# A fused GELU layer and its gradients: the plain loads of the first block, moved from SyncE's DMA queue to GpSimd's

## The chip, the cores and the metric

The kernel runs on one core of a Trainium2 chip. The metric is the device time of one execution in microseconds. All tensors are bf16; products are accumulated in f32.

## The reference

```python
# x [1, 2048, 448], w1 [448, 1792], b1 [1792], w2 [1792, 448], b2 [448], grad_out like x
def _fwd_reference(x, w1, b1, w2, b2):
    h = jnp.einsum("bsd,df->bsf", x, w1) + b1
    h = jax.nn.gelu(h, approximate=True)
    return jnp.einsum("bsf,fd->bsd", h, w2) + b2

_out, _vjp = jax.vjp(_fwd_reference, x, w1, b1, w2, b2)
return (_out, *_vjp(grad_out))     # out, and the gradients of x, w1, b1, w2, b2
```

## The kernel before

The 2048 rows of x are cut into four blocks of 512, and the 1792 hidden features into seven pairs of 128-wide tiles. One step is one pair of one block, so the first part has 28 steps. In a step TensorE makes `pu` (x times w1, transposed: features on partitions) and `pq` (grad_out times w2, transposed); ScalarE and VectorE turn these into `hT` (the GELU) and `ghT` (the gradient at the hidden layer). Out of hT and ghT TensorE also makes the rows of the output and of x's gradient ("units", bank `ps`), which are stored through GpSimd's queue. The second part makes the weight gradients from hT, ghT, x and grad_out; the change does not touch it.

448 is three times 128 plus 64. The last 64 rows of w1 are a tensor of their own on the chip, `wt1`, and the half products with them (line 237) use 64 partitions. For pq, grad_out and w2 are read shifted by 64, so that the half tile comes first.

What each product needs on the chip: `xT` and `gT` (x and grad_out, transposed by the DMA), `w1_f` and `wt1` (w1 as it is), `w2T` (w2 transposed), `w2_sb` (w2 as it is, for the output units) and `w1T_sb` (w1 transposed, for the units of x's gradient). The loads of the first block come in pieces by columns or tiles of the hidden features, because the pairs are taken in the order `FP = [1, 2, 3, 4, 5, 6, 0]`: the first step takes columns 256 to 512, the second 512 to 768, the third 768 to 1024, and the last 0 to 256.

The order of all instructions is written out by hand (`tc.manual_schedule()`): each engine runs its instructions in program order and waits for semaphores. DMAs are issued by three engines in their own queues: SyncE (SP), ScalarE (ACT) and GpSimd (POOL). In the profile q1 is SyncE's DMA queue, q10 ScalarE's and q0 GpSimd's. DMAs of SyncE and ScalarE share eight completion semaphores, so that one waits, before it is issued, until the one eight places back has landed; GpSimd's have eight of their own, used in the same way.

In the kernel before, SyncE issues nearly all loads of the first block, transposes and plain loads interleaved (lines 142 to 168): x's two halves, w1 512:768, w1 768:1024, w2 tiles 2:4, gT, w2T 256:512, and so on up to w1T (line 167) and the second block's gT. ScalarE issues w1 256:512 (line 143). GpSimd issues only b1 (line 139) before the first output rows are ready.

On TensorE the first steps run in this order: pu of step 0 (line 216, and its half product, line 237), pu of step 1, pu of step 2 (w1 768:1024), four pairs of matmuls of output units for step 0 (`pieces`, line 372, with w2 tiles 2:4), the half products of pu of step 2 and of pq of step 0 (line 237: `wt1`, `gT`, `w2T`), the rest of pq of step 0 (line 273), units for step 1, and so on. w1T is first used at step 7 (line 372). VectorE's last instruction of a step, `dve_gh` (line 343), takes pq and writes ghT.

The names in the profile leave out digits: `w_f` is w1_f, `wt` is wt1, `w_sb` is w2_sb, `b_rows` is b1_rows and `b_bc` is b2_bc; a line 121, 122, 125 or 129 is that of the loading helper.

Of the kernel before, what the change touches and what calls it, by code (L numbers as in the profile page):

```python
# [19 lines left out]
def kernel(  # L20
# [15 lines left out]
    nc = tc.nc  # L36
    P = 128
    B, S, D = x.shape
    F = w1.shape[1]
    assert (B, S, D, F) == (1, 2048, 448, 1792)  # L40
    NS = S // P
    NF = F // P
    KF = D // P
    DL = D - KF * P
    SB = 512
# [8 lines left out]
    ROW0 = [SB, 2 * SB, 3 * SB, 0]  # L54
# [4 lines left out]
    x2 = x.rearrange("b s d -> (b s) d")  # L59
# [18 lines left out]
    b2_bc = const.tile([P, D], BF16, name="b2_bc")  # L78
    row0 = const.tile([P, P], BF16, name="row0")
    w1_f = const.tile([P, KF, F], BF16, name="w1_f")  # L80
    w2T = const.tile([P, KF + 1, F], BF16, name="w2T")
    wt1 = const.tile([P, F], BF16, name="wt1")
# [12 lines left out]
    xT, gT = {}, {}  # L95

    def wide(src, r0, n, shift):
        return bass.AP(src.tensor, src.offset + r0 * D - shift, [[D, n], [1, (KF + 1) * P]])

    def load_x(b):  # L100
        t = blk.tile([P, KF + 1, SB], BF16, name="xT", tag="xT")
        r0 = ROW0[b]
        if b in WIDE:
            nc.sync.dma_start_transpose(out=t[:], in_=wide(x2, r0, SB, 0))  # L104
        else:
            nc.sync.dma_start_transpose(out=t[:, 0:KF, :], in_=x2[r0:r0 + SB, 0:KF * P])
            nc.sync.dma_start_transpose(out=t[:, KF, :], in_=x2[r0:r0 + SB, D - P:D])
        xT[b] = t

    def load_g(b):  # L110
        t = blk.tile([P, KF + 1, SB], BF16, name="gT", tag="gT")
        r0 = ROW0[b]
        if b in WIDE:
            nc.sync.dma_start_transpose(out=t[:], in_=wide(g2, r0, SB, DL))  # L114
        else:
            nc.sync.dma_start_transpose(out=t[:, 1:KF + 1, :], in_=g2[r0:r0 + SB, DL:D])
            nc.sync.dma_start_transpose(out=t[:, 0, :], in_=g2[r0:r0 + SB, 0:P])
        gT[b] = t

    def load_w1(eng, f0, f1):  # L120
        eng.dma_start(out=w1_f[:, :, f0:f1], in_=w1[0:KF * P, f0:f1].rearrange("(kt p) f -> p kt f", p=P))  # L121
        eng.dma_start(out=wt1[0:DL, f0:f1], in_=w1[KF * P:D, f0:f1])  # L122

    def load_w2(eng, t0, t1):
        eng.dma_start(out=w2_sb[:, t0:t1, :], in_=w2[t0 * P:t1 * P, :].rearrange("(ft p) d -> p ft d", p=P))  # L125

    def load_w2T(f0, f1):
        if f0 > 0:
            nc.sync.dma_start_transpose(out=w2T[:, :, f0:f1], in_=wide(w2, f0, f1 - f0, DL))  # L129
        else:  # L130
            nc.sync.dma_start_transpose(out=w2T[:, :, 16:f1], in_=wide(w2, 16, f1 - 16, DL))
            nc.sync.dma_start_transpose(out=w2T[:, 1:KF + 1, 0:16], in_=w2[0:16, DL:D])
            nc.sync.dma_start(out=w2T[DL:P, 0, 0:16], in_=w2[0:16, 0:DL].rearrange("f d -> d f"))

    nc.vector.memset(zero[:], 0.0)
    nc.gpsimd.memset(b1_rows[:], 0.0)
# [2 lines left out]
    nc.gpsimd.dma_start(out=b1_rows[0:NF, :], in_=b1.rearrange("(ft p) -> ft p", p=P))  # L139
    xT[0] = blk.tile([P, KF + 1, SB], BF16, name="xT", tag="xT")  # L140
    halves = [slice(0, SB // 2), slice(SB // 2, SB)]
    nc.sync.dma_start_transpose(out=xT[0][:, :, halves[0]], in_=wide(x2, ROW0[0], SB // 2, 0))
    load_w1(nc.scalar, 256, 512)
    nc.sync.dma_start_transpose(out=xT[0][:, :, halves[1]], in_=wide(x2, ROW0[0] + SB // 2, SB // 2, 0))
    warm = stg.tile([P, 1], F32, name="warm", tag="warm", bufs=1)
    nc.scalar.activation(out=warm[:], in_=zero[:, 0:1], func=ACT.Gelu_apprx_tanh)
    load_w1(nc.sync, 512, 768)
    load_w1(nc.sync, 768, 1024)
    load_w2(nc.sync, 2, 4)
    load_g(0)  # L150
    load_w2T(256, 512)
    load_w2(nc.sync, 4, 6)
    load_w1(nc.sync, 1024, 1280)
    load_w2T(512, 768)
    load_w2(nc.sync, 6, 8)
    load_w1(nc.sync, 1280, 1536)
    load_w2T(768, 1280)
    load_w2(nc.sync, 8, 12)
    load_w1(nc.sync, 1536, F)
    load_w1(nc.sync, 0, 256)  # L160
    load_w2(nc.sync, 12, NF)
    load_w2(nc.sync, 0, 2)
    load_w2T(1280, F)
    nc.sync.dma_start(out=b2_bc[:], in_=b2.rearrange("(o d) -> o d", o=1).to_broadcast((P, D)))
    load_x(1)
    load_w2T(0, 256)
    nc.sync.dma_start_transpose(out=w1T_sb[:], in_=w1[:, :])
# [256 lines left out]
    loads = {6: ("x", 2), 8: ("g", 2), 10: ("x", 3), 11: ("g", 3)}  # L424
# [44 lines left out]
    for i in range(1, NSINGLE):  # L469
        f = i + LEAD  # L470
# [271 lines left out]
```

## Time and profile before

| | |
|---|---|
| median of 3 runs | 271.88 us (271.28 to 272.45) |
| the profiled execution | 272.33 us, its span 270.5 us |
| TensorE (PE) busy | 263.7 us, 97% of the span |
| VectorE (DVE), ScalarE (ACT) busy | 176.1 and 139.3 us |
| GpSimd (POOL) busy | 39.7 us |
| DMA queue of SyncE, of GpSimd, of ScalarE | 36.43, 4.27 and 3.44 MB |
| chain that ended last | PE 82%, SyncE's queue 12%, DMA 4% |
| granted TensorE clock | 1.00 |

The profile is one execution. Times in it count from the start of its span. "Busy" leaves out the time of queues: an issue by SyncE ("SPq") has a duration, but is the time in which the queue is taken, and the data lands some microseconds later. In the chain of waits each row is followed back to what released it. A row of waits has the waiting engine, tile and line, then what it waited for, and then the sum in us, the number of waits and the longest one. In a timeline row the bracket tells how long the engine was idle before it, and what ended this.

### The profile page before, as it was taken

The numbers are of one execution on the slowest core, as the hardware profiler recorded it, in microseconds if no ns is written. First come the engines' busy times: TensorE is split into PE (matmuls) and PEld (weight loads), VectorE is DVE, ScalarE is ACT, GpSimd is POOL, SyncE is SP. The second block draws the span as 40 slices with busy tenths as digits, with TensorE's granted clock in tenths as the row PEclk, the third lists the DMA queues.
The fourth block names the chain that finished last, engine by engine and source line by source line (L and its number), as shares of the span: only waits on it lengthen the run. The fifth ranks groups of instructions, "written<-read, shape, count | busy, mean of one in ns | idle before, by whom it ended". The sixth has DMA issues, their size and how long they took to land.

```text
span 270.5 us, 4721 instructions
## 1 busy us (share of the span) xinstructions
PE 263.7 (97%) x1941; PEld 148.0 (55%) x1948; DVE 176.1 (65%) x208; ACT 139.3 (51%) x163; POOL 39.7 (15%) x50
## 2 busy tenths in 40 slices
PE   8999998999999999999999999999999999999995
PEld 7334343444445665555457888874444665555554
DVE  1689999799999779696798930309999992000000
ACT  2898899689995867968676520012111211111111
POOL 1000004011002020110202021221510007900000
PEclk9999999999999999999999999999999999999999
DMA  7999989999999995162642439999311111999851
GB/s 161 207 186 252 180 168 186 252 261 183 250 257 218 266 210 130 61 166 58 168 101 93 78 56 249 368 242 271 92 40 39 41 29 45 195 224 227 202 126 34
DMA packets 112965, 44.44 MB, mean 164 GB/s; under 512 B 92032, under 2 KB 111824, under 8 KB 112944
## 3 DMA queue, kind: packets, MB, share of 16 engines
q1 hardware_dynamic: 106352, 36.43, 63.2%
q0 software_dynamic: 1824, 4.27, 5.2%
q10 hardware_dynamic: 4768, 3.44, 4.1%
q8 instruction: 15, 0.25, 0.4%
q14 instruction: 6, 0.05, 0.1%
HBM read 7.23 MB, written 14.23 MB: 79 GB/s over the span
## 4 chain that ended last, share of the span: by engine, by line
PE 82%; SPq 12%; DMA 4%; issue 1%; ACT 0%
PE ps L237 23%; PE ps_v L694 16%; PE ps_w L662 13%; PE pq L237 9%; PE pu L237 8%; DMA w1T_sb<-in_w_dram 4%; PE ps L372 4%; SPq L129 4%; PE pu L216 3%; PE pq L273 2%; PE ps_w L673 2%; SPq L125 1%; SPq L104 1%; SPq L121 1%; SPq L122 1%; SPq L114 1%
## 5 line engine op out<-in xcount | busy, mean ns | idle before, releaser
L311 ACT ACTIVATE U<-pu,b1T 128x512 bf16<-128x512 f32 x55 | 33.9, 687 | 20.3 <-PE pu L237 20.1
L343 DVE SCALAR_TENSOR_TENSOR ghT<-Z,pq 128x1024 bf16<-128x1024 bf16 x28 | 33.9, 1221 | 14.2 <-PE pq L237 11.5
L386 POOL DMA_DIRECT2D out_dram<-st x32 | 19.1, 602 | 161.4 <-ACT st L383 107.6
L694 PE MATMUL ps_v<-g_nat,h_nat 128*128 128x448 bf16 (+1 forms) x240 | 42.6, 340 | 0.0
L237 PE MATMUL pq<-gT,w2T 64*128 64x512 bf16 x242 | 36.2, 376 | 0.6 <-DMA w2T<-in_w_dram 0.5
L662 PE MATMUL ps_w<-gh_nat,x_nat 128*128 128x512 bf16 (+1 forms) x192 | 36.5, 352 | 0.0
L237 PE MATMUL ps<-w1T_sb,ghT 64*128 64x448 bf16 x336 | 33.9, 349 | 0.0
L694 PEld LDWEIGHTS <-h_nat 128*128 128x128 bf16 x240 | 23.3, 98 | 19.3 <-DMA out_dram<-st 0.3
L237 PE MATMUL ps<-w_sb,hT 64*128 64x448 bf16 x336 | 33.7, 349 | 0.0
L329 ACT ACTIVATE Z<-Z 128x2048 bf16<-128x2048 bf16 (+1 forms) x18 | 27.5, 1528 | 7.7 <-DVE Z L325 7.6
L648 DVE TENSOR_TENSOR acc<-acc,gh_nat 128x1792 f32<-128x1792 f32 x14 | 30.0, 2142 | 0.5
L662 PEld LDWEIGHTS <-x_nat 128*128 128x128 bf16 x192 | 18.7, 98 | 17.9 <-issue 0.4
L237 PEld LDWEIGHTS <-ghT 64*128 64x128 bf16 x336 | 23.5, 94 | 8.7
L320 ACT ACTIVATE A<-U 128x1024 bf16<-128x1024 bf16 (+1 forms) x19 | 27.7, 1457 | 0.7 <-DVE U L313 0.4
L317 ACT ACTIVATE hT<-U 128x1024 bf16<-128x1024 bf16 (+1 forms) x20 | 27.7, 1391 | 0.2
L237 PEld LDWEIGHTS <-hT 64*128 64x128 bf16 x336 | 20.4, 94 | 11.9
L697 ACT CAST st<-ps_v 128x448 bf16<-128x448 f32 (+1 forms) x15 | 7.6, 507 | 34.8 <-PE ps_v L694 34.8
L383 ACT CAST st<-ps 128x448 bf16<-128x448 f32 x20 | 9.8, 532 | 29.0 <-PE ps L237 27.6
L216 PE MATMUL pu<-xT,w_f 128*128 128x512 bf16 (+1 forms) x100 | 22.6, 366 | 0.6 <-DMA xT<-in_x_dram 0.4
L237 PEld LDWEIGHTS <-w2T 64*128 64x128 bf16 x248 | 18.0, 94 | 8.7 <-DMA w2T<-in_w_dram 1.1
L665 ACT CAST st<-ps_w 128x512 bf16<-128x512 f32 (+1 forms) x12 | 6.4, 533 | 28.9 <-PE ps_w L662 28.9
L237 PE MATMUL pu<-xT,w_f 64*128 64x512 bf16 x144 | 20.5, 376 | 0.0
(52 smaller groups left out, 256.0 us busy)
## 6 DMA issues: line engine op xcount, KB each, us to landing
hT_dram<-hT SPq DMA_DIRECT2D x28, 256.0 KB, 3.0
out_dram<-st POOLq DMA_DIRECT2D x32, 112.0 KB, 3.5
x_nat<-in_x_dram SPq DMA_DIRECT2D x1, 1792.0 KB, 9.5
g_nat<-in_grad_out_dram SPq DMA_DIRECT2D x1, 1792.0 KB, 14.4
out_dram<-st ACTq DMA_DIRECT2D x13, 112.0 KB, 3.4
w_f<-in_w_dram SPq DMA_DIRECT2D x6, 192.0 KB, 4.1
out_dram<-st ACTq DMA_DIRECT2D x9, 128.0 KB, 1.7
w_sb<-in_w_dram SPq DMA_DIRECT2D x5, 224.0 KB, 4.2
```

The source lines that it names most:

```text
L129: nc.sync.dma_start_transpose(out=w2T[:, :, f0:f1], in_=wide(w2, f0, f1 - f0, DL))
L216: nc.tensor.matmul(PU[f][a][:, rs], lhsT=w1_f[:, kt, cols(p, a)], rhs=xT[b][:, kt, rs], start=(kt == 0 and rs.start == 0), stop=False, ski ...
L237: mm = nc.tensor.matmul(ps, lhsT=w, rhs=m, start=start, stop=stop, tile_position=(hf.start, 0), skip_group_check=True)
L311: nc.scalar.activation(out=dst, in_=PU[f][a][:], func=ACT.Identity, bias=bias)
L317: nc.scalar.activation(out=rows(hT, r), in_=part(U4, r), func=ACT.Gelu_apprx_tanh)
L320: nc.scalar.activation(out=part(A4, ks), in_=part(U4, ks), func=ACT.Square, scale=math.sqrt(3.0 * GELU_A * GELU_C))
L329: nc.scalar.activation(out=z, in_=z, func=ACT.Tanh, scale=-1.0 / 3.0)
L343: nc.vector.scalar_tensor_tensor(out=rows(ghT, [k]), in0=part(Z4, [k]), scalar=1.0, in1=PQ[k][:], op0=ALU.add, op1=ALU.mult)
L386: nc.gpsimd.dma_start(out=(out2 if self.kind == "o" else gx2)[r:r + P, :], in_=st[:, 0:D])
L648: nc.vector.tensor_tensor(out=v, in0=in0, in1=gh_nat[:, b, :, j, :], op=ALU.add)
L662: nc.tensor.matmul(ps[:, 0:n * P], lhsT=x_nat[:, st_, kt * P:(kt + 1) * P], rhs=gh_nat[:, b, ft0:ft0 + n, j, :], start=(st_ == 0), stop=(s ...
L694: nc.tensor.matmul(ps[:, 0:w], lhsT=h_nat[ft][:, st_, :], rhs=g_nat[:, st_, h * w:(h + 1) * w], start=(st_ == 0), stop=(st_ == NS - 1))
```

## The change

The plain loads from w1 768:1024 onwards leave SyncE's queue and are issued by GpSimd. In front of them stands an empty instruction on GpSimd, which waits until the first half of x has landed. w1's 64 last rows are loaded for columns 768 to 1792 in one DMA instead of four. b2's load and the piece of w2T with 2-byte elements (16 rows, 64 columns) move to the end of GpSimd's list. SyncE's queue is left with the transposes in their old order, and w1 512:768.

```diff
@@ load_w2T
-            nc.sync.dma_start(out=w2T[DL:P, 0, 0:16], in_=w2[0:16, 0:DL].rearrange("f d -> d f"))
@@ the loads of the first block
-    nc.sync.dma_start_transpose(out=xT[0][:, :, halves[0]], in_=wide(x2, ROW0[0], SB // 2, 0))
+    first = nc.sync.dma_start_transpose(out=xT[0][:, :, halves[0]], in_=wide(x2, ROW0[0], SB // 2, 0))
     load_w1(nc.scalar, 256, 512)
...
     load_w1(nc.sync, 512, 768)
-    load_w1(nc.sync, 768, 1024)
-    load_w2(nc.sync, 2, 4)
+    landed = nc.gpsimd.nop()
+    tc.add_manual_dep(landed.ins, first.ins.name, mybir.DependencyInfo(mybir.DependencyClass.Sync, mybir.DependencyReason.DATA),
+                      reason="plain loads behind x")
+    nc.gpsimd.dma_start(out=w1_f[:, :, 768:1024], in_=w1[0:KF * P, 768:1024].rearrange("(kt p) f -> p kt f", p=P))
+    nc.gpsimd.dma_start(out=wt1[0:DL, 768:F], in_=w1[KF * P:D, 768:F])
+    load_w2(nc.gpsimd, 2, 4)
+    load_w2(nc.gpsimd, 4, 6)
+    nc.gpsimd.dma_start(out=w1_f[:, :, 1024:1280], in_=w1[0:KF * P, 1024:1280].rearrange("(kt p) f -> p kt f", p=P))
+    load_w2(nc.gpsimd, 6, 8)
+    nc.gpsimd.dma_start(out=w1_f[:, :, 1280:1536], in_=w1[0:KF * P, 1280:1536].rearrange("(kt p) f -> p kt f", p=P))
+    load_w2(nc.gpsimd, 8, 12)
+    nc.gpsimd.dma_start(out=w1_f[:, :, 1536:F], in_=w1[0:KF * P, 1536:F].rearrange("(kt p) f -> p kt f", p=P))
+    load_w1(nc.gpsimd, 0, 256)
+    load_w2(nc.gpsimd, 12, NF)
+    load_w2(nc.gpsimd, 0, 2)
+    nc.gpsimd.dma_start(out=b2_bc[:], in_=b2.rearrange("(o d) -> o d", o=1).to_broadcast((P, D)))
+    nc.gpsimd.dma_start(out=w2T[DL:P, 0, 0:16], in_=w2[0:16, 0:DL].rearrange("f d -> d f"))
     load_g(0)
     load_w2T(256, 512)
-    load_w2(nc.sync, 4, 6)
-    load_w1(nc.sync, 1024, 1280)
     load_w2T(512, 768)
-    load_w2(nc.sync, 6, 8)
-    load_w1(nc.sync, 1280, 1536)
     load_w2T(768, 1280)
-    load_w2(nc.sync, 8, 12)
-    load_w1(nc.sync, 1536, F)
-    load_w1(nc.sync, 0, 256)
-    load_w2(nc.sync, 12, NF)
-    load_w2(nc.sync, 0, 2)
     load_w2T(1280, F)
-    nc.sync.dma_start(out=b2_bc[:], in_=b2.rearrange("(o d) -> o d", o=1).to_broadcast((P, D)))
     load_x(1)
     load_w2T(0, 256)
     nc.sync.dma_start_transpose(out=w1T_sb[:], in_=w1[:, :])
```

## The prediction

> **What bounds the kernel now.** The page's first lines say that TensorE is busy for 97% of the span, so only its waits can be won. I asked for these waits, and they are short:
>
> ```profile
> PE 263.7 (97%) x1941; PEld 148.0 (55%) x1948; DVE 176.1 (65%) x208; ACT 139.3 (51%) x163; POOL 39.7 (15%) x50
> PE ps L372 <- DMA w1T_sb<-in_w_dram: 1.1, 1, 1.1
> PE pq L237 <- DMA w2T<-in_w_dram: 0.5, 2, 0.3
> PE pu L216 <- DMA xT<-in_x_dram: 0.4, 1, 0.4
> ```
>
> The 6.8 us in which TensorE is not busy are mostly start and end. DMA waits that the change can touch are w1T (1.09 us, ending at 46.05) and two for w2T (0.24 and 0.28, at 13.05 and 18.47): **1.61 us in all, the most it can win**. x's own wait stays, since nothing ahead of it moves. The chain of waits shows why w1T is late: from 0.7 to 34.5 us it runs through SyncE's queue, issue after issue with 0.04 us between. The queue is bound by issuing, and the transposes stand behind the plain loads:
>
> ```profile
> 4.70 0.58 SPq L121
> 5.86 0.59 SPq L125
> 6.49 2.84 SPq L114
> 9.37 1.30 SPq L129
> ...
> 33.84 0.66 SPq L133
> 34.54 11.47 DMA w1T_sb<-in_w_dram
> ```
>
> When data is needed I read from TensorE's timeline (start, duration, line): the first users of w1 columns 768 to 1024, of w2 rows 2:4, and of gT with the first w2T part.
>
> ```profile
> 9.51 1.47 PE L216 MATMUL pu<-xT,w_f 128*128 128x512 bf16 x6
> 10.82 1.68 PE L372 MATMUL ps<-w_sb,hT 128*128 128x448 bf16 x8
> 13.05 0.39 PE L237 MATMUL pq<-gT,w2T 64*128 64x512 bf16 x1 [0.24 <-DMA w2T<-in_w_dram]
> ```
>
> By the DMA view, narrowed to these issues, w1 768 is issued at 4.70 and lands 3.4 us later (8.1, 1.4 us early); w2 2:4 is issued at 5.86 and lands 3.6 later (9.4, also 1.4 early). So the early plain loads have 1.4 us of slack, and the two early w2T parts have none.
>
> **The change, part by part.** *Off SyncE.* 18 plain issues leave its queue; their durations in the chain of waits (0.46 to 0.66 each) sum to 9.7 us, with 18 gaps of 0.04 to 10.4 us. gT moves from 6.49 to 4.70, the first w2T part from 9.37 to about 7.6, the next from 12.39 to 8.9, and w1T from 34.54 to about 24.1. With its 11.47 us, w1T lands near 36. Even if GpSimd's loads held the transposes up for 9 us it would land at 45, when TensorE comes for it (44.96). So the 1.09 goes in nearly every case. The w2T waits go too, if the transposes flow freely. SyncE's waits for its eight completion semaphores now refer to the transposes eight back, which have landed by then: nothing.
>
> What comes next if these waits go? VectorE. Its ghT instruction (L343) starts every 5.17 us from 20.51 to 46.37, while TensorE's step there takes 4.75. But the first two of them wait for TensorE themselves (0.21 and 0.48), so the chain moves with it, and at 50.11 TensorE has 2.5 us in hand over the L343 that ended at 47.59. I count the 1.61 as winnable in full.
>
> *Onto GpSimd.* Its queue is empty from 1.95 to 42.85 us, so 15 issues fit; the output stores at 42.85 wait behind them only if they take over 2.4 us each, against 0.54 to 0.67 in the rows. TensorE, ScalarE and VectorE keep their order. The added wait is for x's first half, whose landing lets TensorE start at 5.64; GpSimd thus issues w1 768 at about 5.65, 0.95 us later than SyncE did. All fourteen other moved loads queue behind this wait. wt follows at 6.3 and w2 2:4 at 6.9 (from 5.86). What do GpSimd's transfers take to land? The nearest rows are its own, under transposes and without:
>
> ```profile
> out_dram<-st POOLq DMA_DIRECT2D x32, 112.0 KB, 3.5
> wt<-in_w_dram POOLq DMA_DIRECT2D x1, 224.0 KB, 6.0
> w2T<-w2T POOLq DMA_DIRECT2D x1, 224.0 KB, 6.6
> ```
>
> Singly, the stores at 42.85 to 45.89 and 55.62, beside transposes, took 3.3 to 5.1 (middle 4.3); at 109 and 120, with the queues quiet, 2.0. The bounds for w1 768 are thus 5.65 + 2.0 = 7.7 and 5.65 + 6.0 = 11.7, against a need at 9.51: no loss to 2.2 us. I take 4.3, since x, w1 and gT are moving then, and 0.3 for 192 KB instead of 112 (the transposes alone move 290 GB/s from 9.5 to 10.5 us): 10.25, so TensorE waits 0.75. w2 2:4 then lands at 6.9 + 4.3 + 0.4 = 11.6, or up to 12 behind the two loads ahead of it; it is needed at 10.82 + 0.75 = 11.6. **Stall: 1.0 us** (bounds 0 and 2.5). The later plain loads have room: TensorE takes about 450 KB each 4.75 us, 94 GB/s; w1 1024, issued near 8.2, is needed at 16.4. b2 and the 2-byte piece of w2T are not needed before 39 and 43.
>
> VectorE could hold up GpSimd's issues. At 86.27 and 97.73, beside a 0.68 us TENSOR_SCALAR, an issue took 0.95 instead of 0.54; beside the 0.43 us ones of the first block, 0.63 and 0.67. I used the latter; two long ones ahead of w2 2:4 would add 0.6. [...]
>
> *Sum.* The profiled execution took 272.33 (span 270.5 and 1.8 around it), 0.45 above the median of 271.88. 272.33 - 1.61 + 1.0 = 271.7, and by the median 271.3. Half a percent is 1.36 us, about what a measurement here can tell from none: 270.5 to 273.2.
>
> **The rivals.** *Starved transposes (slower).* GpSimd issues 2.8 MB at some 200 KB each 0.6 us, faster than the 290 GB/s at which they can move. If its queue keeps the DMA engines while it has work, gT's rest and the first w2T part, 0.5 MB, wait. The DMA view for two windows in which both queues had work, 47.0 to 47.8 and the longer 45.4 to 52.3:
>
> ```profile
> q0 software_dynamic: 117, 0.31, 98.1%
> q1 hardware_dynamic: 97, 0.02, 11.4%
> ```
> ```profile
> q1 hardware_dynamic: 3612, 0.91, 62.4%
> q0 software_dynamic: 274, 0.92, 47.5%
> ```
>
> q0 is GpSimd's and q1 SyncE's. Within a burst the transposes get 6% of the bytes; over seven microseconds they get half. Which of the two holds for a load of 10 us decides. Starting at 5.65 + 2.2 = 7.9 (the delay until the first packet, as I take it from queues with some load), 2.8 MB at 290 GB/s end at 17.8. At a share near 0 the w2T part lands at 17.8 + 1.7 + 0.9 = 20.4, a stall of 7.3 over 13.05: 272.33 - 0.45 - 1.61 + 7.3 = 277.6. At a quarter of 290 it lands near 15.7, a net loss of 1; at half, near 12.3, no loss. It decides below a fifth: 273.3 to 277.6. [...]
>
> *Late plain loads (slower).* The 6.0 us row holds for the first ones: w2 2:4 at 13 or later, stalls of 2.5 to 4: 272.8 to 274.3. In its favour: 192 to 224 KB is that row's size. Against: those transfers stood behind four stores.
>
> *All on time (faster).* At the 2.0 us of the quiet rows, or up to 3.8, w1 768 is there by 9.5, and nothing is paid: 270.3. Against it: DMA is busy 95% from 5.6 to 13.1.
>
> *Nothing changes.* The program as built has the loads in GpSimd's queue and the wait in front of the first, so I give this no chance of its own.
>
> **How the numbers follow.** My sum: 0.45 (own range 270.5 to 273.2). Starved transposes 0.30 and late plain loads 0.12, counted slower. All on time 0.13. So faster 0.13, same 0.45, slower 0.42. The range runs from the full gain, 270.4, to most of the starved case, 276.8; it leaves out perhaps 2 in 10, at both ends.
>
> **What would show it.** Right: the wait for w1T at 46 is gone and w1T lands before 40; GpSimd's first load starts at 5.65; TensorE waits 0.5 to 1.5 us in all for w1 or w2 between 9.5 and 12. Wrong: a wait of over 3 us at the first pq L237 for w2T or gT, with q0 alone in the DMA view from 9 to 17 us; or no new wait at all. A GpSimd issue well over 0.7 us would break the landing sums and, by thinning the burst, the starved case with them.

## The result: slower by 4.5%, and the profile after

The changed kernel takes 284.14 us (median of four, 283.23 to 285.7) against 272.16 for the kernel before beside it (271.28 to 272.55): a ratio of 1.045, with a 95% interval of 1.040 to 1.051. The prediction was 271.3 with a range to 276.8. It was wrong, on the side of its rival "starved transposes" and past that rival's upper end of 277.6. The profiled execution took 284.29, its span 282.5, against 272.33 and 270.5: 12.0 us are to be found.

The page's busy times and TensorE's waits, of the changed kernel:

```profile
PE 267.1 (95%) x1941; PEld 148.4 (53%) x1948; DVE 176.5 (62%) x208; ACT 139.7 (49%) x163; POOL 50.2 (18%) x65
PE pq L241 <- DMA w2T<-in_w_dram: 7.8, 2, 6.4
PE pu L220 <- DMA w_f<-in_w_dram: 2.5, 1, 2.5
```

The wait for w1T is gone, as are the two short ones for w2T. Three others stand in their place. TensorE's timeline (start, duration, what; in brackets the idle time before) shows where:

```profile
11.75 2.74 PE L220 MATMUL pu<-xT,w_f 128*128 128x512 bf16 x6 [2.47 <-DMA w_f<-in_w_dram]
27.78 0.60 PE L241 MATMUL pq<-gT,w2T 64*128 64x512 bf16 x1 [6.40 <-DMA w2T<-in_w_dram]
36.33 0.39 PE L241 MATMUL pq<-gT,w2T 64*128 64x512 bf16 x1 [1.38 <-DMA w2T<-in_w_dram]
```

The first is for w1 768:1024, on GpSimd's queue. The other two are for the second and the third part of w2T, which SyncE issues. The chain of waits, in order of time, has SyncE issue early and the data come very late:

```profile
4.70 2.24 SPq L114
6.99 2.10 SPq L129
9.13 3.24 SPq L129
12.41 23.87 DMA w2T<-in_w_dram
```

gT was issued at 4.70 and landed at 12.14; the first w2T part was issued at 6.99 and landed at 15.76, in time for TensorE. The second, issued at 9.13, landed at 27.73; the third, issued at 12.41, at 36.29. GpSimd's own last piece landed at 36.11.

What the waits cost besides their length is in the windows (from:to, length, busy times of PE, PEld, DVE, ACT and POOL, then the granted clock, DMA share and GB/s):

```profile
11.75:14.50 2.75, 2.75 (x7) 1.05 (x8) 2.47 (x5) 2.47 (x3) 2.14 (x3) 0.50 1.09 241
21.40:27.78 6.38, 0.00 (x1) 0.01 (x2) 1.76 (x4) 0.69 (x1) 0.00 (x0) 0.80 1.09 93
27.78:31.50 3.72, 3.39 (x9) 1.16 (x11) 0.00 (x0) 3.04 (x4) 0.00 (x0) 0.50 1.26 107
31.50:36.30 4.80, 3.45 (x15) 1.34 (x13) 4.54 (x8) 1.28 (x2) 0.00 (x0) 0.94 1.32 72
```

After the first two waits the clock stands at half (0.50): six matmuls of pu take 2.74 us there, against 1.47 in the kernel before. By the granted clock TensorE's 2.75 and 3.39 us of work there would have taken half as long, 3.1 us lost. The half clock lasts a little beyond these rows, until 14.98 and 32.04, with TensorE busy: 0.5 us more, 3.6 in all. Waits 2.47 + 6.40 + 1.38 = 10.25; plus 3.6; less the 1.61 that the change did remove and x's wait of 0.37, which this execution does not have: 11.9 of the 12.0.

The same windows show what lies behind the long wait: from 21.4 to 36.3 us all queues together move 72 to 107 GB/s, with a DMA share of 1.09 to 1.32. The DMA view tells the stretch before from this one (bytes and share of each queue, q0 GpSimd's and q1 SyncE's, 9 to 17 and 21.4 to 27.78 us):

```profile
DMA packets 2362, 2.00 MB, mean 249 GB/s; under 512 B 1966, under 2 KB 2015, under 8 KB 2362
q0 software_dynamic: 501, 1.53, 87.0%
q1 hardware_dynamic: 1861, 0.46, 28.5%
```
```profile
DMA packets 886, 0.60 MB, mean 93 GB/s; under 512 B 772, under 2 KB 797, under 8 KB 886
q0 software_dynamic: 147, 0.41, 62.8%
q1 hardware_dynamic: 739, 0.19, 45.8%
```

While GpSimd's list is full, 249 GB/s move and the transposes get 23% of the bytes. When its list runs out, both queues crawl. In the packet records a 4480-byte packet of GpSimd's, whose median over the trace is 0.20 us, takes 2.3 us on average from 21.5 to 23.0 (14 packets).

### The profile page after: what moved, and what is told of

Read it like the earlier page. It is cut to its first block, busy times and chain, and to the rows that moved or that the text cites. A ratio compares the mean times of both kernels' runs of the same rounds, so it can differ in the third digit from the quotient of the medians.

```text
span 282.5 us, 4723 instructions
## 1 busy us (share of the span) xinstructions
PE 267.1 (95%) x1941; PEld 148.4 (53%) x1948; DVE 176.5 (62%) x208; ACT 139.7 (49%) x163; POOL 50.2 (18%) x65
## 3 DMA queue, kind: packets, MB, share of 16 engines
q0 software_dynamic: 2832, 7.14, 10.3%
## 4 chain that ended last, share of the span: by engine, by line
PE 86%; DMA 8%; SPq 4%; issue 0%; ACT 0%
PE ps L241 22%; PE ps_v L698 15%; PE ps_w L666 13%; PE pq L241 9%; PE pu L241 9%; DMA w2T<-in_w_dram 8%; PE ps L376 6%; PE pu L220 5%; PE pq L277 5%; PE ps_w L677 2%; SPq L129 2%; SPq L114 1%; SPq L141 0%; SPq L143 0%; PE ps L380 0%
## 5 line engine op out<-in xcount | busy, mean ns | idle before, releaser
L241 PEld LDWEIGHTS <-hT 64*128 64x128 bf16 x336 | 20.3, 94 | 11.9
L220 PE MATMUL pu<-xT,w_f 128*128 128x512 bf16 (+1 forms) x100 | 23.9, 381 | 2.8 <-DMA w_f<-in_w_dram 2.5
```

The costliest lines, as they stand in the source:

```text
L220: nc.tensor.matmul(PU[f][a][:, rs], lhsT=w1_f[:, kt, cols(p, a)], rhs=xT[b][:, kt, rs], start=(kt == 0 and rs.start == 0), stop=False, ski ...
L241: mm = nc.tensor.matmul(ps, lhsT=w, rhs=m, start=start, stop=stop, tile_position=(hf.start, 0), skip_group_check=True)
```

## The experiments

In the expectations, theory 1 is the rival "starved transposes", theory 2 "late plain loads", and theory 4 says that GpSimd's loads and SyncE's transposes block each other while both have work. Theory 3 says that any second queue with plain loads holds the transposes up, and theory 5 that it is the length of the other queue's packets. Where one time is given, it is a single execution, beside the kernel before in the same job (271.9 to 272.7); the kernel before itself ranges from 270.6 to 273.3, so a difference of about 1 us in a single execution says nothing.

### Parts of the change

**First pieces back on SyncE** (against the changed kernel):

```diff
     load_w1(nc.sync, 512, 768)
+    load_w1(nc.sync, 768, 1024)
+    load_w2(nc.sync, 2, 4)
...
-    nc.gpsimd.dma_start(out=w1_f[:, :, 768:1024], ...)
-    nc.gpsimd.dma_start(out=wt1[0:DL, 768:F], in_=w1[KF * P:D, 768:F])
-    load_w2(nc.gpsimd, 2, 4)
+    nc.gpsimd.dma_start(out=wt1[0:DL, 1024:F], in_=w1[KF * P:D, 1024:F])
```

> The changed kernel with w1 768:1024 and w2 2:4 (and their piece of wt) back in SyncE's queue, where the kernel before has them; the other loads stay with GpSimd behind x. Theory 1 (GpSimd's queue, while it has loads waiting, takes the DMA engines away from SyncE's transposes): the wait of 2.5 us for w1 at 9 to 12 us goes, with its stretch at half clock, but w2T 512:768 and 768:1280 still land late, TensorE waits 5 to 9 us for w2T, 278 to 281 us. Theory 2 (GpSimd's transfers are slow to land, and the late first ones are what shifts all that follows): with the first two back no long wait is left, 271 to 274 us.

284.2 us. The wait for w1 is gone, but TensorE waits once for w2T, 11.8 us until 24.42. With the late plain loads taken away the time is the same, so theory 2 falls. Theory 1 priced it too low as well (278 to 281): gT landed at 19.32 and the first w2T part at 24.38, later than in the changed kernel (12.14 and 15.76).

**No wait ahead of GpSimd's list:**

```diff
-    landed = nc.gpsimd.nop()
-    tc.add_manual_dep(landed.ins, first.ins.name, ...)
```

> The changed kernel without the wait for x's first half: GpSimd's first load is issued at about 2 us. Theory 4: x's own transposes are caught as well; x lands after 7 us instead of 5.3 to 5.8, TensorE starts later, w1 768 still lands after 9 us, and the waits for w2T stay over 6 us: 284 to 292 us. Rival (the loads are only late, by the wait and by GpSimd's slow start): everything of GpSimd lands some 3.5 us earlier, the wait for w1 goes, 278 to 282 us.

290.6 us: x's halves land at 6.84 and 9.61 instead of 5.30 and 5.80 in the changed kernel (3.5 us of waits), gT at 23.5, and the wait for w2T is 11.8 us. GpSimd's loads, started earlier, held up more of the transposes.

**GpSimd's list held back in groups**, each behind the landing of a w2T part:

```diff
     load_w2(nc.gpsimd, 4, 6)
+    gate(t0)      # an empty GpSimd instruction that waits for the first w2T part
...
     load_w2(nc.gpsimd, 6, 8)
+    gate(t1)      # and so on: t1, t2, t3 are the next parts of w2T
...
```

> The changed kernel, but GpSimd's list is held at four places: after w1 768, wt, w2 2:4 and w2 4:6 it waits for the landing of w2T 256:512, then issues two loads and waits for w2T 512:768, then two and waits for w2T 768:1280, then four and waits for w2T 1280:1792. Theory 1: the transposes are delayed by two or three loads at a time instead of fifteen, so the waits for w2T shrink from 7.8 us to under 2, while the first wait for w1 (2.5 us) and its half clock stay: 274 to 277 us. Theory 2: every load is issued later than in the changed kernel and takes as long to land, so plain loads come late as well: 284 us or more.

276.91 us. Fewer loads beside transposes, less loss. TensorE still waits 0.7 for w1 and 1.6 for w2T, with half clock behind it from 16.95 to 20.37, and a plain load held back by its gate comes late (a wait of 1.9 for w2).

**The two small pieces at the end of GpSimd's list back on SyncE** (b2's row and the 2-byte piece of w2T, in their old places):

```diff
-    nc.gpsimd.dma_start(out=b2_bc[:], ...)
-    nc.gpsimd.dma_start(out=w2T[DL:P, 0, 0:16], ...)
     load_w2T(1280, F)
+    nc.sync.dma_start(out=b2_bc[:], ...)
     load_x(1)
     load_w2T(0, 256)
+    nc.sync.dma_start(out=w2T[DL:P, 0, 0:16], ...)
```

> The changed kernel, but with b2's row and the 2-byte piece of w2T back in their old places on SyncE's queue; the twelve larger plain loads stay on GpSimd's. If the slow stretch from 21.5 to 36 us in the changed kernel comes from these two loads, the last in GpSimd's list: 277 to 280, and transposes land at their usual pace from about 22 us on. If it comes from the large loads and the transposes alone: 282 to 285, with a joint rate of 150 GB/s or less for at least 6 us and a wait of over 3 us for w2T.

280.73 us, between the two expectations. The long wait for the second w2T part stays (6.2 us, until 26.32), with 136 GB/s from 17 to 23 us; but GpSimd's last load is in at 26.56, and from there the transposes run as usual, at 288 GB/s from 27 to 29. So the large loads alone block, and the small pieces stretch it: in this execution the second w2T part landed 1.5 us earlier (26.27 against 27.73), the wait of 1.38 for the third part was gone, and the time was some 3 us shorter.

### Four loads, 1.1 MB

The kernel before, with w2 4:6, w1 1024:1280, w2 6:8 and w2 8:12 taken off SyncE's queue. On GpSimd's, behind x (`eng` is nc.gpsimd, and then nc.scalar):

```diff
     load_w2(nc.sync, 2, 4)
+    load_w2(eng, 4, 6)
+    eng.dma_start(out=w1_f[:, :, 1024:1280], ...)
+    load_w2(eng, 6, 8)
+    load_w2(eng, 8, 12)
     load_g(0)
     load_w2T(256, 512)
-    load_w2(nc.sync, 4, 6)
-    load_w1(nc.sync, 1024, 1280)
+    nc.sync.dma_start(out=wt1[0:DL, 1024:1280], ...)
...
-    load_w2(nc.sync, 6, 8)
...
-    load_w2(nc.sync, 8, 12)
```

> The kernel before, with the same four loads (w2 4:6, w1 1024:1280, w2 6:8, w2 8:12) moved to GpSimd's queue behind x's first half. Theory 1: 1.1 MB take about 4 us, in which the transposes nearly stand still; gT or w2T 256:512 lands 3 to 4 us late and TensorE waits 2 to 4 us: 274 to 277 us. Theory 2 (slow landing of what TensorE needs first): none of the four is needed before 14.9 us, so nothing waits: 270.5 to 272.5 us.

On ScalarE's, ahead of its first work:

> The kernel before, with only w2 4:6, w1 1024:1280, w2 6:8 and w2 8:12 (1.1 MB) moved, to ScalarE's queue, issued at about 3.5 to 7.5 us. Theory 1 in the form 'it is GpSimd's packets of 4 KB against 256 bytes': ScalarE's packets are single rows of 512 or 896 bytes, so the transposes keep a quarter or more of the bytes and w2T lands at most 2 us late: 271 to 274 us. Theory 3 (any second queue with plain loads holds the transposes up): as slow as its partner run on GpSimd, 275 to 278 us.

On ScalarE's, right behind `copy_u(0)`, so that they lie beside gT and w2T:

> The kernel before, with the same four loads issued by ScalarE at 8.2 to 10 us, right after its first U copy, while gT and w2T 256:512 are on their way from SyncE at their old times. ScalarE loses about 1.8 us there. Theory 4 in the form 'only GpSimd's queue does it': w2T 256:512 lands by 15 us, TensorE waits 2 us at most for w2T, 272 to 275 us, and the DMA engines move 200 GB/s and more from 8 to 16 us. Theory 3 (any second queue beside transposes): throughput falls to 120 GB/s, w2T lands near 20, 279 to 282 us.

On GpSimd's, with gT and all that follows on SyncE held until the last of the four has landed:

```diff
+    last = load_w2(nc.gpsimd, 8, 12)
+    held = nc.sync.nop()          # waits for `last`
     load_g(0)
```

> The kernel with the four loads on GpSimd (e2b), but SyncE holds gT and all later transposes until the last of the four has landed, so that loads and transposes are never beside each other. Theory 4 (GpSimd's loads and SyncE's transposes, when both have work, block each other, and together move about 110 GB/s instead of 290): alone, the 1.1 MB land by 10 to 12 us, gT and w2T then take their usual 4 to 6 us and land by 18; TensorE waits 4 to 5 us for w2T, less than the 7.9 us of e2b although the transposes start 5 us later: 275 to 278 us. Rival (GpSimd's loads are slow by themselves, and what follows waits for them): they land near 19 us as in e2b, TensorE waits 11 us or more, 283 us and up.

Measured: 281.05 on GpSimd beside the transposes, past theory 1's range; 275.37 and 276.87 on ScalarE; 278.16 on GpSimd with the transposes behind. TensorE's wait for w2T in the first, third and fourth:

```profile
PE pq L241 <- DMA w2T<-in_w_dram: 7.9, 1, 7.9
PE pq L234 <- DMA w2T<-in_w_dram: 2.6, 1, 2.6
PE pq L244 <- DMA w2T<-in_w_dram: 5.5, 1, 5.5
```

On GpSimd's queue beside the transposes, 12 to 18 us moves 112 GB/s, gT lands 13.5 us after its issue, and the four loads at 10.3 to 19.8. One after the other, the same loads move 330 GB/s from 9 to 11 us and the last lands at 12.74, then gT takes 4.5 us: holding the transposes back entirely is some 3 us better than letting both run. That the loads are slow by themselves (the rival there, 283 and up) is excluded, though the time and the wait of 5.5 came out just above what theory 4 gave.

On ScalarE's queue the same loads beside the same transposes move 284 GB/s from 10.5 to 14.5 us. The DMA view tells the two apart (packets, MB and share; q10 is ScalarE's), GpSimd's run from 12 to 18 us and then ScalarE's from 10.5 to 14.5:

```profile
q1 hardware_dynamic: 1028, 0.26, 81.4%
q0 software_dynamic: 122, 0.41, 41.7%
```
```profile
q10 hardware_dynamic: 1401, 1.06, 98.6%
q1 hardware_dynamic: 340, 0.08, 16.9%
```

ScalarE's loads also keep the transposes waiting, with 7% of the bytes left for them, but they keep their pace and are through by 15.31; w2T lands at 16.27. On GpSimd's queue the loads crawl too, and w2T lands at 20.86. The ScalarE run still loses 4.2 us, so neither forecast for it holds (272 to 275, 279 to 282): w2T came 1.3 us later than theory 4 allowed, TensorE waited 0.9 for ScalarE's hT, and after the wait of 2.6 us the clock was at half from 16 to 22. The earlier ScalarE run, at 275.37, lies in theory 3's range, but tells less, because there x was late (1.2 us of waits) and SyncE could not issue gT before 9.21; it moved 244 to 316 GB/s from 6 to 12 us.

So by these single executions about half of the 8.6 us on GpSimd's queue is any queue's price for 1.1 MB beside the transposes, and half is the crawl. About 3 us in both are half clock, behind the wait (5.83 and 6.16 us of TensorE's work).

### One load, 448 KB

w2 8:12 alone moved, to GpSimd behind x, and its twin with ScalarE behind `copy_u(0)`:

```diff
-    load_w2(nc.sync, 8, 12)
+    load_w2(nc.gpsimd, 8, 12)     # first kernel, behind the wait for x
...
     copy_u(0, "av")
+    load_w2(nc.scalar, 8, 12)     # the twin
```

> The kernel before, with a single load, w2 8:12 (448 KB), moved to GpSimd's queue behind x's first half. In proportion to its bytes: 448 KB at 290 GB/s delay the transposes by 1.5 us, TensorE waits under 1.5 us for w2T, 271.5 to 273.5 us. Theory 4: while the load lasts it moves some 75 GB/s and lands 6 us or more after its first packet; gT and w2T land 3 to 5 us late, 274 to 277 us.

> Twin of the single load on GpSimd's queue (275.85): the kernel before with w2 8:12 (448 KB) taken from SyncE's queue and issued by ScalarE, right after copy_u(0). If GpSimd's queue is the cause (theory 4): gT lands at 12 to 13.5, no jam, 271.5 to 273. If any move of this load out of SyncE's order costs the time: 275 or more.

275.85, and 272.0 for the twin, a ratio of 1.000 to the kernel before (0.997 to 1.003 by the interval). Here the end of a GpSimd load is seen alone. The DMA view of the GpSimd run from 10.5 to 12.4 us (its first line is GB/s in 40 slices):

```profile
GB/s 65 75 54 49 65 32 38 22 16 5 0 0 0 0 0 0 94 0 0 0 94 0 0 0 100 0 0 5 154 0 0 5 170 0 0 43 59 11 16 22
DMA packets 134, 0.06 MB, mean 30 GB/s; under 512 B 128, under 2 KB 129, under 8 KB 134
q1 hardware_dynamic: 127, 0.03, 61.1%
q0 software_dynamic: 7, 0.02, 3.1%
```

Seven packets of GpSimd's are left, from the middle on one about every 0.2 us, and almost nothing moves between them, though gT is not done. The trace has sixteen reports of completion for each of SyncE's loads: of w2 2:4, ahead of gT, fifteen had come at 9.52 and the last at 12.20. So in this run one part of the load lagged by 2.7 us, and gT first reported at 14.34. That the part is one of the sixteen DMA engines is the author's reading; the trace does not say which engine a report is from. TensorE waited 1.17 for w2 2:4, 2.27 for w2T, and then ran at half clock from 17.49 to 20.90, 1.7 of the 3.2 us lost.

The twin is not free of it: 118 GB/s from 10.5 to 12.4, gT at 14.38 (12 to 13.5 expected) and a wait of 2.28. But w2 2:4 was in time, no half clock followed, and the waits for w1T and w2T of the kernel before were gone, so it came out even: its time was forecast rightly, the way to it was not.

Is it the length of the packets? 448 KB that nobody needs (128 rows of w1, to a place in `gh_nat` that is written again later), added to the kernel before:

```diff
+    nc.scalar.dma_start(out=<128 rows of 3584 bytes>, in_=w1[0:P, :])            # behind copy_u(0)
+    nc.scalar.dma_start(out=<the same, in pieces of 512 bytes>, in_=w1[0:P, :])  # second kernel
+    nc.gpsimd.dma_start(out=<128 rows of 3584 bytes>, in_=w1[0:P, :])            # third, behind x
```

> Beside everything that the kernel before does, ScalarE's queue loads 448 KB more right after copy_u(0): 128 rows of w1, each 3584 bytes in one piece, to a place that nothing reads before it is written again. It lies beside gT and the first w2T. Theory 5 (a 256-byte packet of a transpose takes its turn with a whole packet of the other queue, and all engines' transposes go at the pace of the engine with most of the other queue's packets left, so it is the length of the packets that jams them, whichever engine issues): gT lands 14 us or later, the time is 275 to 277. Theory 4 (only GpSimd's queue jams the transposes): the load costs its own 1.6 us of DMA time (448 KB at 290 GB/s), gT lands 12.5 to 13.7, the time is 273 to 274.5, as with short rows.

> The same 448 KB on ScalarE's queue at the same place, but written in pieces of 512 bytes, seven for each row. Both theories: no jam; the load costs at most its own 1.6 us of DMA time, gT lands 12.5 to 13.7, the time is 272.7 to 274.5. If it jams as the long rows do (gT 14 or later, 275 or more), the length of the packets is not what decides.

> The same 448 KB in rows of 3584 bytes, issued by GpSimd behind x's first landing, with everything of the kernel before left on its queue. Both theories: as with the single load moved to GpSimd (275.85), gT lands 14 to 16, the time is 275 to 277.5. If GpSimd's queue does more than long packets do, this is slower than the same rows on ScalarE's queue by 1 us or more.

272.21, 271.67 and 276.64, with 272.29 for the kernel before. ScalarE's long rows and short rows cost nothing that can be told from none, less than either theory gave (gT at 13.14 and 13.47; 333 GB/s with the long ones from 10.5 to 12.4), so packets of 3584 bytes do not block by their length, and theory 5 falls. The same bytes on GpSimd's queue cost 4.4 us: w2 2:4 at 11.71 and a wait of 0.91, w2T 1.53, and w1T 1.96 with half clock behind it (49.26 to 52.68, 1.7 of the 4.4). Here no single report lagged: all sixteen reports of w2 2:4 came between 11.62 and 11.71.

One difference besides the queue is left in these pairs: GpSimd issued its load earlier (5.76 against 8.27 and 7.51, and 5.98 against 7.47 for the twins), and no run has the same load on ScalarE's queue at 5.8. Later loads on GpSimd's queue are slow as well: behind the gates, those issued at 16.64 to 22.22 took 9 to 14 us to land.

A store in place of the load (SBUF to device memory, 448 KB), and a quarter of the load (112 KB), both on GpSimd's queue and added to the kernel before:

```diff
+    nc.gpsimd.dma_start(out=side[:], in_=<3584 bytes a partition of xT[0]>)            # side: in device memory
+    nc.gpsimd.dma_start(out=<128 rows of 896 bytes>, in_=w1[0:P, 0:F // 4])            # second kernel
```

> The kernel before, and GpSimd stores 448 KB more from SBUF (the first 3584 bytes a partition of xT of block 0) to device memory, where nothing reads it, behind x's landing. If all traffic of GpSimd's queue jams the transposes, as its load of the same size did (276.64): 275.5 to 278, gT at 14 or later. If only loads do: 272 to 274, gT at 12 to 13.7.

> As the extra load of 448 KB on GpSimd's queue (276.64), but a quarter of it: 112 KB, 128 rows of 896 bytes. If the jam lasts as long as GpSimd's queue has packets beside a transpose: a quarter of the 4.4 us, 273 to 274. If it is a fixed price of one load on that queue: 275.5 to 277.

272.31 and 272.95, beside 272.07. The store went through at 340 GB/s together with the rest from 8 to 10 us, its sixteen reports came within 0.2 us, and gT landed at 12.79. The quarter came out 0.9 us above, no more than single executions differ. That rules out a fixed price for each load (275.5 to 277); that the price goes with the bytes fits, but is not shown.

### What was left to win

The 2-byte piece of w2T and b2's row issued by ScalarE at two idle places, and nothing else changed:

```diff
         if i > 1:
             act_tanh([i])
+        if i == 2:
+            nc.scalar.dma_start(out=w2T[DL:P, 0, 0:16], ...)
+        if i == 3:
+            nc.scalar.dma_start(out=b2_bc[:], ...)
```

> The kernel before, with only the 2-byte piece of w2T (256 elements of 2 bytes a row) and b2's row taken from SyncE's queue and issued by ScalarE in iterations 2 and 3, where it is idle; all other loads stay. The hole of some 2 us in the DMA traffic ahead of w1T goes, and w1T is issued about 1.3 us sooner: the wait of 1.09 us for w1T goes. If that wait was worth its length and nothing else comes late: 270.8 to 271.6 against the kernel before in the same job (0.996 to 0.9985 of it). If another wait takes its place: no change.

272.49, a ratio of 1.0015 (0.9995 to 1.0035): no gain. w1T is issued at 33.20 instead of 34.54 and its wait is gone, but TensorE waits 0.6 for w2T and 0.5 for VectorE's ghT elsewhere. No version was measurably faster than the kernel before.

## Why the prediction was wrong, step by step

*SyncE's issues.* gT was issued at 4.70 as worked out, the next two at 6.99 and 9.13 (7.6 and 8.9 predicted). From there SyncE's queue was held up: one issue took 13.0 us, and w1T was issued at 40.90, not 24.1, and landed at 49.52, past the bound of 45. TensorE was late enough by then not to need it before 57.9.

*The 1.61 us that can be won.* The waits did go. But the step "I count the 1.61 as winnable in full" falls with the ScalarE version above: w1T's wait of 1.09 went there, and the time stayed.

*The stall for plain loads, 1.0 us.* GpSimd's first load was issued at 5.59 (5.65 predicted) and landed at 11.71: 10.25 was taken, and 11.7 was the upper bound. TensorE waited 2.47 instead of 0.75, and 1.6 more went to half clock. The row taken, single stores, was too short a neighbour (and the middle of the five that it names took 4.75, not 4.3). The 6.0 us of the row with a load of like size beside transposes came nearer, but the same first load took 5.19 with the small pieces back on SyncE and 4.83 in the gated list, so the 6.1 here is the upper end of what it takes.

*The rest of the plain loads had room*: right, TensorE waited for none, though they took up to 17 us.

*The half share* is the step that failed: what GpSimd's loads cost the transposes was put at nothing. The sum rests on the transposes getting half the bytes, read from 45.4 to 52.3 us of the kernel before. In that stretch GpSimd's queue carried four stores of 112 KB, one load of 224 KB and an on-chip copy of as much. A store did not block where the load did (272.31 against 276.64), so the stretch was no measure for fifteen loads in a row; but the one load in it did not make the queues crawl either (222 GB/s from 49 to 53.6 us). The rival's working for a quarter of the bandwidth was close on what it priced: 23% in the trace, and the first w2T part at 15.76 against 15.7 predicted, which TensorE, late itself, did not wait for. By that working 23% gives some 273.5 us. (Its "below a fifth: 273.3" does not follow from it: a fifth gives 274.6.) The rest, over 10 us, is mostly what neither the sum nor the rival had: they priced the first w2T part alone, and the rival let GpSimd's 2.8 MB end at 17.8 at 290 GB/s. In truth the joint rate fell to 93 and the last piece came at 36.11; the second part of w2T made the long wait, and the third another. The short window of the kernel before, 6% of the bytes, was no measure either.

*The signs named beforehand.* GpSimd's first load started as named. The others did not come as named: the wait for w1T was gone, but w1T landed at 49.52 and not before 40. The long wait was at the second part of w2T, not at the first pq, and from 9 to 17 us q0 was not alone.

*One queue holding up another.* From 9 to 17 us the transposes have 23% of the bytes and 1861 of the 2362 packets, neither the half of the sum nor the share near 0 of the rival. That GpSimd's queue held up the transposes, as the rival has it, is borne out.

*The clock*, which the sum leaves out, cost 3.6 us. It was 0.50 from 11.56 to 14.98 and from 25.22 to 32.04 us, at the waits of 2.47 and 6.40. What length of wait brings it is not shown: in the gated list one of 1.63 was followed by half clock (16.95 to 20.37), with the extra load on GpSimd one of 1.96 (49.26 to 52.68, a mean of 0.67 in the row below), while in the twin on ScalarE the clock stayed at 1.00 after one of 2.28:

```profile
48.69 4.50 PE L376 MATMUL ps<-w1T_sb,ghT 128*128 128x448 bf16 x14 [1.96 <-DMA w1T_sb<-in_w_dram]
50.00:54.00 4.00, 4.00 (x15) 1.79 (x14) 3.25 (x7) 0.12 (x1) 0.00 (x0) 0.67 1.15 278
```
```profile
15.10 0.39 PE L236 MATMUL pq<-gT,w2T 64*128 64x512 bf16 x1 [2.28 <-DMA w2T<-in_w_dram]
15.00:17.00 2.00, 1.91 (x10) 0.78 (x11) 0.00 (x0) 1.57 (x3) 0.00 (x0) 1.00 1.22 314
```

*VectorE's hold on GpSimd's issues.* No issue of the list took over 0.85 us; the 0.95 of the row at 86.27 was not reached.

*What stays open.* Why GpSimd's loads crawl beside transposes, and a store or ScalarE's rows do not, is not shown; a single late report is in one run, and another that lost more does not have it. Nor is it shown why ScalarE's w2 8:12 slowed the joint rate to 118 GB/s and its rows of w1 did not, or why the one GpSimd load at 46.43 in the kernel before did no harm.

## What to carry to other kernels

Be wary of loads on GpSimd's queue where DMA transposes that TensorE is about to need run beside them: 448 KB cost 3 to 4 us here, 1.1 MB 8.6, and the whole list 12, while on ScalarE's queue 448 KB cost nothing and 1.1 MB 4.2. Before bandwidth shares are read from a trace, see that both queues do there what they will do after the change, loads against loads, and price the end of the list, not only its first consumer. A wait on TensorE can be paid again in clock: waits of 1.6 to 2.5 us cost up to 1.7 more here, longer ones 1.7 to 3.1.

## What the runs showed of the hardware

- GpSimd's loads and SyncE's transposes together moved 249 GB/s while the list of fifteen was full (9 to 17 us) and 72 to 107 when it ran out; 112 with four loads (12 to 18 us), and 30 at the end of a single one (10.5 to 12.4). Apart, they moved 330 (the four loads, 9 to 11 us, transposes held) and 290 (the kernel before, 9.5 to 10.5 us).
- ScalarE's four loads and the same transposes together moved 284 GB/s (10.5 to 14.5 us), and the loads left 7% of the bytes to the transposes.
- A 448 KB store on GpSimd's queue at the same place came out 0.2 us above the kernel before, within its spread; the load 4.4.
- The first data packet of GpSimd's list moved 3.8 us after its issue (5.59 to 9.36), with transposes and SyncE's loads ahead of it.
- A granted clock of 0.50 came with waits of 2.47 and 6.40 us in the changed kernel, of 1.63 in the gated list and of 1.96 with the extra load on GpSimd's queue; after one of 2.28, in the twin on ScalarE, the clock was 1.00.
